# Chunked attention before a squared-ReLU FFN: transposed scores, softmax sums from a ones column, 64x64 matmuls on four tiles, and attention placed at fixed steps of the preceding block's FFN

## Chip, cores and metric

One core of a Trainium2 chip. The metric is the device time of one execution in microseconds (us). Several executions are timed and their median is quoted. Ratios with an interval are the mean time of one kernel's fast runs over the mean of the kernel before's fast runs of the same rounds, so they are not quite the ratio of the medians quoted beside them.

Names: PE is the matrix engine TensorE (PEld its weight loads), DVE is VectorE, ACT is ScalarE, POOL is GpSimd. SP issues the DMAs. A stretch of a profile is written 126.05–158.09, in us from the start of the profiled execution. The granted clock is the share of its full clock that PE was given, as the profile records it; matmuls at half of it are called cold. The head is the time before the FFN runs steadily.

## The reference

```python
# q, k, v: (batch 8, heads 8, sequence 576, dim 64), float32
# chunks of 64 tokens: 9 per sequence; each attends to itself only
scores = matmul(q_c, k_c^T) / sqrt(64)
attn   = exp(scores - max); attn = attn / (sum(attn) + 1e-9)
x      = matmul(attn, v_c)              # -> (4608 tokens, 512)
h      = maximum(x @ w_in, 0)           # w_in  (512, 2048)
out    = (h * h) @ w_out                # w_out (2048, 512), float32 out
```

The FFN is 9 blocks of 512 tokens with 128 matmuls of 128x128 by 128x512 each. Attention is small beside it, but it consists of many small instructions that depend on each other.

## The kernel before

A batch has 576 tokens, and four head pairs. Attention runs in groups: for each head pair one group of eight chunks and one of a single chunk. After each group three queued FFN units are emitted. A scheduler places instructions where the program leaves it a choice.

```python
groups = [(0, 8), (8, 1)]
# ... pools, weights: w_in by DVE/ACT, w_out by GpSimd, cut ...

def attention_group(b, hp, tiles, c0, nch):
    # 8 (or 2) transposes of q and k, then a copy to qkT: cut
    for cc in range(nch):                       # scores, queries on partitions
        nc.tensor.matmul(out=sc_ps[0:64, cc],   lhsT=qkT[0:64, 0, cc],   rhs=qkT[0:64, 1, cc], ...)
        nc.tensor.matmul(out=sc_ps[64:128, cc], lhsT=qkT[64:128, 0, cc], rhs=qkT[64:128, 1, cc], ...)
    nc.scalar.activation(out=attn_exp[:, :nch], in_=sc_ps[:, :nch], func=AF.Exp, scale=scale)
    nc.vector.reduce_sum(out=sums[:, :nch], in_=attn_exp[:, :nch], axis=AXL.X)
    nc.vector.reciprocal(out=rec[:, :nch], in_=sums[:, :nch])
    nc.vector.tensor_tensor(out=attn_n[:, :nch], in0=attn_exp[:, :nch], in1=rec..., op=ALU.mult)
    for cc in range(nch):                       # the weights of attention, turned
        nc.tensor.transpose(out=attnT_ps[0:64, cc * 128:(cc + 1) * 128], in_=attn_n[:, cc], ...)
    nc.vector.tensor_copy(out=attnT[:, :nch], in_=attnT_ps[0:64])
    for cc in range(nch):                       # values, two tiles
        # two 64x64 matmuls into xTo_ps[0:64] and xTo_ps[64:128]: cut
    nc.scalar.copy(out=xT[:, hp, t0:t0 + T], in_=xTo_ps)

# ffn_chunk_units(j): 16 units "4 matmuls w_in, relu, square", then 4 units "16 matmuls w_out, copy, store"

for b in range(B):
    # ... loads, cut ...
    for hp in range(n_hp):
        for (c0, nch) in groups:
            attention_group(b, hp, tiles, c0, nch)
            if hp == n_hp - 1:
                # queue the units of every FFN chunk whose 512 tokens are now complete
                ...
            emit_pending(3)
```

The softmax here doesn't subtract the row's maximum and nothing guards it: scores larger than these inputs give would overflow.

## Time and profile before

| | before |
|---|---|
| time, median of 3 runs | 428.6 us (427.62 to 429.38) |
| profiled span | 427.9 us |
| PE busy, share of the span | 85% |
| mean granted PE clock | 0.931 |
| steady FFN begins (read from the timeline) | about 49 us |
| period: 576 tokens of attention and one FFN chunk | 44.45 us |

The lines of the profile are in the prediction below. The "busy" column counts an engine as busy while one of its instructions is in flight, and matmuls are pipelined, so the 85% does not say that only 15% is to be had. At the 216 ns between starts that the prediction reads from the tail, a block's 128 matmuls take 27.64 us.

### The profile page before, as it was taken

What the parts mean: (1) busy time and instruction counts of PE and PEld (TensorE: products, weight loads), DVE (VectorE), ACT (ScalarE), POOL (GpSimd) and SP (SyncE); (2) the same over time, 40 slices, a digit from 0 to 9 for tenths busy, and PEclk for the clock granted to TensorE, in tenths of its full rate; (3) what the DMA queues carried; (4) which work ended last, traced back from release to release, by engine and by line L of the source; (5) the groups of instructions that cost most, each with busy time, mean ns of one, the idle gap of its engine ahead of it and who ended that gap; (6) DMA issues with size and microseconds to landing.
All of it is one profiled execution on the core that took longest, in us unless ns stands there. A gap on an engine that the chain in (4) does not pass through costs nothing.

```text
span 427.9 us, 7535 instructions
## 1 busy us (share of the span) xinstructions
PE 365.1 (85%) x2862; PEld 184.5 (43%) x2912; DVE 187.0 (44%) x482; ACT 148.3 (35%) x295; POOL 10.9 (3%) x23
## 2 busy tenths in 40 slices
PE   0256699957999799979997999899988999799996
PEld 0234344433445444444444444444444444344442
DVE  2433444344643565256624572447244734440320
ACT  0111262222532263225422542255224523361631
POOL 0003500000000000000000000000000000000000
PEclk9999999965999699979998899979996999699999
DMA  9966860565314741656045524562356011001001
GB/s 271 285 142 221 240 126 28 133 163 127 80 37 122 171 109 25 170 138 146 19 126 141 129 56 116 138 151 54 90 135 147 23 38 64 0 2 74 25 26 74
DMA packets 123812, 46.64 MB, mean 109 GB/s; under 512 B 116608, under 2 KB 116608, under 8 KB 123264
## 3 DMA queue, kind: packets, MB, share of 16 engines
q1 hardware_dynamic: 123200, 41.97, 39.5%
q10 hardware_dynamic: 576, 4.19, 2.6%
q8 instruction: 23, 0.38, 0.4%
q14 instruction: 13, 0.11, 0.1%
HBM read 36.70 MB, written 9.44 MB: 108 GB/s over the span
## 4 chain that ended last, share of the span: by engine, by line
PE 78%; SPq 5%; DVE 5%; DMA 5%; ACT 3%; issue 2%; ACTq 0%
PE hT L204 33%; PE o_ps L219 26%; PE abank L168 6%; PE abank L122 3%; PE abank L138 3%; PE abank L178 3%; PE abank L129 2%; DMA v_sb<-in_v_dram 2%; DMA k_sb<-in_k_dram 2%; DVE attnT L174 2%; DVE attn_n L160 2%; ACT xT L191 2%; PE abank L184 1%; SPq L97 1%; SPq L100 1%
## 5 line engine op out<-in xcount | busy, mean ns | idle before, releaser
L204 PE MATMUL hT<-xT,w_in_bf 128*128 128x512 bf16 x549 | 149.6, 410 | 8.1 <-ACT xT L191 4.3
L219 PE MATMUL o_ps<-w_out_bf,gT 128*128 128x512 bf16 x553 | 133.2, 380 | 1.9 <-issue 0.6
L211 ACT ACTIVATE rl<-hT 128x512 bf16<-128x512 f32 x130 | 77.6, 597 | 72.1 <-PE hT L204 71.1
L212 DVE TENSOR_TENSOR gT<-rl 128x512 bf16<-128x512 bf16 x144 | 59.8, 420 | 68.4 <-ACT rl L211 68.3
L204 PEld LDWEIGHTS <-w_in_bf 128*128 128x128 bf16 x576 | 55.4, 104 | 67.5 <-issue 21.8
L219 PEld LDWEIGHTS <-gT 128*128 128x128 bf16 x576 | 52.1, 98 | 57.1
L135 DVE COPY qkT<-abank 128x1024 bf16<-128x1024 bf16 x64 | 29.0, 454 | 82.5 <-PE abank L129 82.4
L226 ACT COPY o_sb<-o_ps 128x512 f32<-128x512 f32 x36 | 21.1, 585 | 84.9 <-PE o_ps L219 73.2
L168 PE MATMUL abank<-ident_bf,attn_n 128*64 128x128 bf16 x288 | 31.3, 254 | 17.4 <-DVE attn_n L160 17.4
L156 ACT ACTIVATE attn_exp<-abank 128x512 bf16<-128x512 f32 x64 | 26.0, 410 | 54.2 <-PE abank L144 52.6
L191 ACT CAST xT<-abank 128x512 bf16<-128x512 f32 x64 | 24.5, 399 | 52.7 <-PE abank L184 52.7
L174 DVE COPY attnT<-abank 64x1024 bf16<-64x1024 bf16 x64 | 27.9, 447 | 26.6 <-PE abank L168 26.6
L122 PE MATMUL abank<-ident_bf,q_sb 128*128 128x128 bf16 (+1 forms) x160 | 21.0, 239 | 18.1 <-DMA q_sb<-in_q_dram 13.1
L158 DVE TENSOR_REDUCE sums<-attn_exp 128x8 f32<-128x512 bf16 x64 | 28.2, 444 | 17.4 <-ACT attn_exp L156 17.0
L168 PEld LDWEIGHTS <-attn_n 128*64 128x64 bf16 x288 | 22.1, 128 | 30.9 <-DVE attn_n L160 27.7
L160 DVE TENSOR_TENSOR attn_n<-attn_exp,rec 128x512 bf16<-128x512 bf16 x64 | 28.9, 456 | 1.6
L178 PE MATMUL abank<-attnT,v_sb 64*64 64x64 bf16 x288 | 20.8, 210 | 8.4 <-DVE attnT L174 7.8
L122 PEld LDWEIGHTS <-q_sb 128*128 128x128 bf16 (+1 forms) x160 | 13.5, 108 | 30.6 <-issue 23.6
L138 PE MATMUL abank<-qkT 64*64 64x64 bf16 x288 | 21.6, 204 | 5.3 <-DVE qkT L135 5.1
L138 PEld LDWEIGHTS <-qkT 64*64 64x64 bf16 x288 | 14.5, 114 | 22.4 <-DVE qkT L135 20.2
L178 PEld LDWEIGHTS <-v_sb 64*64 64x64 bf16 x288 | 16.2, 122 | 17.7 <-issue 15.6
L129 PE MATMUL abank<-ident_bf,k_sb 128*128 128x128 bf16 (+1 forms) x160 | 22.7, 235 | 0.0
(17 smaller groups left out, 125.3 us busy)
## 6 DMA issues: line engine op xcount, KB each, us to landing
v_sb<-in_v_dram SPq DMA_DIRECT2D x64, 144.0 KB, 3.2
out_dram<-o_sb SPq DMA_DIRECT2D x36, 256.0 KB, 2.1
q_sb<-in_q_dram SPq DMA_DIRECT2D x64, 128.0 KB, 2.8
k_sb<-in_k_dram SPq DMA_DIRECT2D x64, 128.0 KB, 2.9
w_in_stage<-in_moe_w_in_dram ACTq DMA_DIRECT2D x4, 1024.0 KB, 6.6
w_out_stage<-in_moe_w_out_dram SPq DMA_DIRECT2D x16, 256.0 KB, 3.7
q_sb<-in_q_dram SPq DMA_DIRECT2D x64, 16.0 KB, 2.4
k_sb<-in_k_dram SPq DMA_DIRECT2D x64, 16.0 KB, 2.1
```

What stands on the lines that cost most here:

```text
L122: nc.tensor.transpose(out=qkT_ps[:, sg * 128:sg * 128 + tk], in_=q_bfv[0:tk, sg0 + sg, :, 1::2], identity=ident_bf[0:tk, 0:tk],)
L129: nc.tensor.transpose(out=qkT_ps[:, T + sg * 128:T + sg * 128 + tk], in_=k_bfv[0:tk, sg0 + sg, :, 1::2], identity=ident_bf[0:tk, 0:tk],)
L138: nc.tensor.matmul(out=sc_ps[0:64, cc], lhsT=qkT[0:64, 0, cc], rhs=qkT[0:64, 1, cc], start=True, stop=True,)
L160: nc.vector.tensor_tensor(out=attn_n[:, :nch], in0=attn_exp[:, :nch], in1=rec[:, :nch].to_broadcast([128, nch, CH]), op=ALU.mult,)
L168: nc.tensor.transpose(out=attnT_ps[0:64, cc * 128:(cc + 1) * 128], in_=attn_n[:, cc], identity=ident_bf[0:128, 0:128],)
L174: nc.vector.tensor_copy(out=attnT[:, :nch], in_=attnT_ps[0:64])
L178: nc.tensor.matmul(out=xTo_ps[0:64, cc * 64:(cc + 1) * 64], lhsT=v_bfv[:, 0, c, 1::2], rhs=attnT[:, cc, 0], start=True, stop=True,)
L191: nc.scalar.copy(out=xT[:, hp, t0:t0 + T], in_=xTo_ps,)
L204: nc.tensor.matmul(out=hT, lhsT=w_in_bf[:, dt, ft * 128:(ft + 1) * 128], rhs=xT[:, dt, t0:t0 + TCH], start=(dt == 0), stop=(dt == n_dt - 1),)
L211: nc.any.tensor_scalar(out=rl, in0=hT, scalar1=0.0, scalar2=None, op0=ALU.max)
L212: nc.vector.tensor_tensor(out=gT[:, ft, :], in0=rl, in1=rl, op=ALU.mult)
L219: nc.tensor.matmul(out=o_ps, lhsT=gT[:, ft, tt * 128:(tt + 1) * 128], rhs=w_out_bf[:, ft, :], start=(ft == 0), stop=(ft == n_ft - 1),)
```

## The change

The intent, part by part:

- Scores are computed transposed (keys on partitions), so that their exponentials are already the stationary operand of the values matmul. The 36 transposes per 576 tokens of attention's weights go away.
- V gets a 65th column of ones. The values matmul then yields the softmax sum as well. The division comes after it, on 256 elements instead of 512, and the separate sum goes.
- The 64x64 matmuls use all four 64x64 tiles of the PE array, not the two on the diagonal.
- Tokens are taken in blocks of 512, across batches, so the one-chunk groups vanish.
- The order is fixed by hand. Each block's attention is seven steps at fixed places among the 32 FFN steps of the block before it.

The diff at its core (loads, transposes of q and k, and the FFN bodies are cut, and most removed lines with them):

```diff
-    groups = [(0, 8), (8, 1)]
+    ps_ffn = ctx.enter_context(tc.tile_pool(name="ps_ffn", bufs=4, space=bass.MemoryType.PSUM))
+    ps_att = ctx.enter_context(tc.tile_pool(name="ps_att", bufs=2, space=bass.MemoryType.PSUM))
+    ctx.enter_context(tc.manual_schedule())
...
+    v_tiles = [w_pool.tile([128, n_tt, H, D + 1], FP32, name=f"v_sb{i}") for i in range(2)]
+    for vt in v_tiles:
+        nc.gpsimd.memset(vt[:, :, :, D:D + 1], 1.0)
...
+    wst_pool = ctx.enter_context(tc.tile_pool(name="wst", bufs=2))       # load_w_in, load_w_out:
+            eng = nc.vector if h == 0 else nc.gpsimd                      # halves of a w_in tile
+        eng = nc.vector if i % 2 == 0 else nc.gpsimd                      # whole w_out tiles
...
+    def scores(j, r):
+            for hh in range(2):
+                for t in range(n_tt):
+                    for a in range(2):
+                        for p in range(2):
+                            c = p ^ a
+                            o0 = a * 512 + hh * 256 + t * 64
+                            nc.tensor.matmul(
+                                out=ps[64 * c:64 * c + 64, o0:o0 + 64],
+                                lhsT=qkT[64 * a:64 * a + 64, 1, hh, cols],
+                                rhs=qkT[64 * a:64 * a + 64, 0, hh, cols], ...)
+            nc.scalar.activation(out=e..., in_=ps, func=AF.Exp, scale=scale)
+    def values(j, t):
+            for hp in range(n_hp):
+                e = state[j, "e", hp // 2]
+                for a in range(2):
+                    for p in range(2):
+                        c = p ^ a
+                        nc.tensor.matmul(
+                            out=ps[64 * p:64 * p + 64, a, hp * (D + 1):(hp + 1) * (D + 1)],
+                            lhsT=e[64 * c:64 * c + 64, a, hp % 2, t, :],
+                            rhs=vb[64 * c:64 * c + 64, t, 2 * hp + a, 1::2], ...)
+            nc.vector.reciprocal(out=rec, in_=o[:, :, :, D])
+            # x = o * rec, one tensor_tensor for each a
...
+    def attention(j):
+        return [[transpose_qk(j, 0)], [transpose_qk(j, 1)],
+                [scores(j, 0), scores(j, 1)],
+                [values(j, 0), values(j, 1)], [values(j, 2), values(j, 3)],
+                [transpose_x(j, 0)], [transpose_x(j, 1)]]
...
+    load_qk(0); load_v(0)            # then 4x load_w_in, 8x load_w_out, load_qk(1), load_v(1)
+    # attention(0) runs alone, then for every block j:
+        at = [14, 17, 20, 23, 26, 29, 31] if j == 0 else [1, 4, 8, 13, 17, 22, 26]
+        # before FFN step at[i], step i of attention(j + 1) is issued
```

In `scores`, the four matmuls of one turn of the loop over `t` use the tiles (row group, column group) = (0,0), (0,1), (1,1), (1,0). I call them a quad.

## The prediction

> **What bounds the kernel now.** I read the page first, then the tail and one period of the middle in stretches, then the instruction order of both programs. The page:
>
> ```profile
> span 427.9 us, 7535 instructions
> PE 365.1 (85%) x2862; PEld 184.5 (43%) x2912; DVE 187.0 (44%) x482; ACT 148.3 (35%) x295; POOL 10.9 (3%) x23
> ...
> PE   0256699957999799979997999899988999799996
> ...
> PEclk9999999965999699979998899979996999699999
> DMA  9966860565314741656045524562356011001001
> ...
> L204 PE MATMUL hT<-xT,w_in_bf 128*128 128x512 bf16 x549 | 149.6, 410 | 8.1 <-ACT xT L191 4.3
> L219 PE MATMUL o_ps<-w_out_bf,gT 128*128 128x512 bf16 x553 | 133.2, 380 | 1.9 <-issue 0.6
> ```
>
> TensorE is the bound: no other engine passes 44%. But it has gaps in the first five slices (53 us), and the clock row dips about once every four slices. The durations of 410 and 380 ns overlap each other; what a matmul costs is the distance between starts. That comes from the tail, where only FFN runs: four output evacuations start at 414.05, 417.51, 420.96 and 424.46, so 16 matmuls take 3.455-3.47 us, 216 ns each at full clock. 1152 of them are 248.8 us: the floor that the change doesn't touch. About 179 us lie outside it.
>
> The middle repeats every 44.45 us (one batch of 576 tokens and one FFN chunk). Columns of the stretches: length, busy time of PE, PEld, DVE, ACT, POOL with instruction counts, granted clock, DMA share, GB/s.
>
> ```profile
> 227.80:230.00 2.20, 2.20 (x26) 1.00 (x24) 1.64 (x6) 0.70 (x2) 0.00 (x0) 1.00 0.43 145
> 230.00:234.80 4.80, 2.29 (x33) 1.86 (x32) 2.74 (x9) 1.06 (x4) 0.00 (x0) 0.70 0.75 167
> 234.80:238.70 3.90, 3.67 (x14) 1.88 (x15) 1.36 (x3) 1.06 (x3) 0.00 (x0) 0.50 0.37 85
> 238.70:272.25 33.55, 33.18 (x275) 15.96 (x278) 16.14 (x41) 13.93 (x28) 0.00 (x0) 1.00 0.43 104
> ```
>
> For 4.8 us no FFN unit is left (24 slots per batch, 20 units), and attention runs as a bare chain:
>
> ```profile
> 230.96 0.21 PE L144 MATMUL abank<-qkT 64*64 64x64 bf16 x1
> 231.79 1.05 PE L168 MATMUL abank<-ident_bf,attn_n 128*64 128x128 bf16 x9 [0.62 <-DVE attn_n L160]
> 233.50 0.21 PE L178 MATMUL abank<-attnT,v_sb 64*64 64x64 bf16 x1 [0.67 <-DVE attnT L174]
> ...
> 234.81 0.58 PE L204 MATMUL hT<-xT,w_in_bf 128*128 128x512 bf16 x1 [0.62 <-ACT xT L191]
> ```
>
> The clock then stays at half until 238.7. So 44.45 = 27.6 (128 matmuls) + 4.8 (hole) + about 2 (half of the 3.9 cold us) + 10 of attention on PE while warm.
>
> Inside attention the starts give the costs: eight row-tiled 64x64 pairs take 0.05 us for the first step and then 31.7 ns per pair (202.69 to 202.88 in six steps); the start of such a group is about 0.11 us late after FFN, and FFN about 0.10 us late after it: 0.21 us per switch there and back. Four 128x128 transposes take 0.23 us, 57 ns each.
>
> **What the skill says.** "TensorE: Matmul & The Clock Gate", Back-to-back issue gap, gives N/2.4 + 2.5 ns warm: 215.8 at N=512 and 55.8 at 128. The trace agrees (216, 57). The same section's sustained 131 ns for N=512 isn't seen in the tail. Part 1 there: idleness of some 3.4 us halves the clock; seen at 231.9 (0.50 granted). "TensorEngine Tiling (Array Packing)", Tiling Modes, gives four independent 64x64 tiles, and a drain when the mode changes; the 0.21 us is that drain's price here. The clock-gate page's Part 3 says that a weight load overlaps running matmuls only if its row group differs. No trace of before has two tiles of one row group; the new scores have (each quad goes row 0, row 0, row 1, row 1), so this is my main doubt on PE.
>
> **The change part by part.**
>
> *Removed:* per 576 tokens, 36 transposes of the weights of attention, the sum, the normalisation of 128x512 (DVE 0.68 each) and the evacuations between; the one-chunk groups (nine chunks as 8+1), each with its own mode switch; the hole and its cold stretch, since each block's attention is now spread over fixed slots of the preceding block's 32 FFN steps.
>
> *Added per 512 tokens, on PE:* 48 transposes of 128x128 (32 for q and k, 16 for x) x 57 ns = 2.74 us. 128 small matmuls = 32 quads. If a quad costs what a pair did: 1.0 us; if tiles still go two by two: 2.0. I take 50 ns, 1.6 us. Mode switches: scores of both rounds together, values twice, 3 x 0.21 = 0.63. Sum 5.0; with a little waiting, 5.2.
>
> *Does anything hold PE in a steady block of 27.6 + 5.2 = 32.8 us?* ACT: 16 relu x 0.60 + 4 stores x 0.585 + 2 exp of 128x1024 (from 0.223 at 64 and 0.596 at 512 elements, 0.83 ns each, so 1.02) = 14.0. The two exps make a lump of 2.04 us, and four FFN banks hold 3 x 0.86 us: no stall. DVE: 16 squares x 0.42, four copies of 1024 x 0.69, four values (0.2 reciprocal + 2 x 0.42), two xT copies x 0.69 = 15.0. Between values at slots 13 and 17 DVE has 2.1 + 3 x 0.42 = 3.4 us of work in 3.5 us, and the banks come free before the last squares. DMA: 3.15 MB of q, k, v at 225 GB/s (262.00 to 262.50: share 0.98, 225 GB/s) = 14 us, plus 1 MB out, of 32.8. Hidden. So PE alone paces the blocks.
>
> *The head, on the path.* In the new program's DVE order all eight weight casts stand before the first qkT copy. So attention of block 0 waits for nearly all weights. q, k, v first: 1.3 + 14.0 = 15.3 us. w_in, 4 MB through two 1 MB buffers: about 13.5, as w_out took 34.2 to 48 us in before, with 1 MB in flight too; w_out again 14: 43; the last cast, 44. Then bare: two copies 1.4, scores cold 0.9, exps to 4.8, four values paced by DVE at 1.04 each and their first matmuls to 9.5, two x transposes and copies to 11.2. FFN starts at 55 us.
>
> *Sum:*
> - head 55.0
> - block 0: 27.6 + 2.2 cold + 5.2 + 0.9 (the last x transpose is in its last slot, so the copy to xT is waited for) = 35.9
> - blocks 1 to 7: 7 x 32.8 = 229.6
> - block 8, no attention left: 27.6
> - from the last matmul to the end, as in before (424.4 to 427.9): 3.5
> - measured time over profiled span, as in before: 0.7
>
> 352.3; I say 353.
>
> Against before: 7 periods lose about 11.6 us each, 81 us; the two FFN chunks that ran alone at the end now lie over attention, but the last block still does; the head gets some 6 us worse (steady FFN began at 49).
>
> **The rivals.**
>
> 1. *Quads don't overlap.* If same-row tiles serialise, a quad costs 100 to 130 ns: 32 quads are 3.2 to 4.2 us instead of 1.6, 8 blocks: +13 to +21, about 370. For: the row-group sentence. Against: in before, loads of 110 ns already run at 31.7 ns a pair, so loads are deeply pipelined.
> 2. *The head becomes longer.* V rows now lie 65 floats apart, so its 256-byte pieces land at odd addresses; if they cost double, +5 us; staging waits may add 5: 363. For: PE, DVE and ACT all stand idle in it. The other way, if weights stream at the 385 GB/s seen at 228.5, the head is 6 us shorter: 347.
> 3. *The in-order streams of a fixed order couple.* A late exp or values copy now stops FFN too, at seven points a block. 1 us per block gives +8: 361. Against: each consumer is four slots, 3.5 us, behind its producer.
> 4. *It hardly gains* (over 420), if PE's gaps were the same work elsewhere. The 4.8 us hole, the cold 3.9 us and the counts speak against it.
>
> **Range and chances.** The blocks are fixed by 216 ns x 1152; what is open is 4.2 to 7.5 us of attention per block (-8 to +18) and the head (-6 to +9), not all at once. 342 to 368. Even all rivals together stay under 400. Faster 0.98.
>
> **What would show it right or wrong.** Each step has its line: FFN's first matmul near 55 us and DVE's first qkT copy near 44; a period near 32.8 us; PE's row at 9s from slice 7 on and PEclk without dips after the head; small matmuls by fours 30 to 65 ns apart; DMA share near 0.5. Wrong would be: PE waiting each block on ACT exp or DVE x; quads over 100 ns; the clock below 1.00 in mid-run; q and k of a later block arriving late.

## The result and the profile after

| | before | after |
|---|---|---|
| time, median of 4 runs in the same rounds | 428.99 us | 350.84 us (350.12 to 351.37) |
| ratio, 95% interval | | 0.8176 [0.8149, 0.8203] |
| profiled span | 427.9 us | 349.6 us |
| mean granted PE clock in the profiled run | 0.931 (records from 54.5 us on) | 1.000 (records from 63.6 us on) |
| first FFN matmul after which FFN goes on | about 49 us | 58.14 us |
| period | 44.45 us per 576 tokens | 32.04 us per 512 tokens |

The time fell by 18%. The prediction had 353. One of the other three runs lists a mean clock of 0.936 at the same time, 350.60 us, so the two means don't compare whole runs: time without a record counts as full clock.

The page of the changed kernel. The rows of digits are the span in 40 slices of 8.7 us, as tenths of busy time or of clock:

```profile
span 349.6 us, 6592 instructions
PE 293.8 (84%) x2693; PEld 149.9 (43%) x2736; DVE 132.1 (38%) x314; ACT 123.0 (35%) x199; POOL 11.6 (3%) x17
...
PE   0400026999999999999999999999999999999995
...
PEclk9999999999999999999999999999999999999999
...
L240 PE MATMUL ps_ffn<-xT,w_in_bf 128*128 128x512 bf16 x552 | 131.8, 385 | 2.9 <-DVE xT L215 1.6
...
L162 PE MATMUL ps_att<-qkT 64*64 64x64 bf16 x576 | 7.0, 199 | 35.0 <-DVE qkT L147 35.0
```

From slice 7 on (counted from 0), PE's row is all 9s but for the last, and the dips of the clock row are gone. In the slices before, the clock row says nothing: its first record is at 63.6 us, and full clock is printed up to there. The share of busy time is the same as before, 84% against 85%: this column could not have told the gain. What is left of idle time stands in slices 0 to 6. Its largest part is in the last line: 35.0 us in which PE waits for the copy of the transposed q and k.

The changed kernel by stages. Columns: length, busy time of PE, PEld, DVE, ACT and POOL with counts, granted clock, DMA share, GB/s:

```profile
0.00:58.14 58.14, 9.23 (x177) 6.87 (x178) 13.00 (x26) 3.33 (x3) 11.56 (x17) 1.00 0.89 234
58.14:94.01 35.87, 34.45 (x298) 16.85 (x304) 14.35 (x34) 13.34 (x22) 0.00 (x0) 1.00 0.59 124
126.05:158.09 32.04, 31.78 (x301) 16.24 (x305) 13.98 (x34) 13.45 (x22) 0.00 (x0) 1.00 0.60 132
```

The first is the head, the second block 0, and the third a steady block. DVE and ACT are busy 14 of 32 us and DMA 60%, so nothing but PE fills a steady block. All blocks from 1 to 7 last 32.03 to 32.11 us.

The order of PE within that steady block, from the timeline. Columns: start, length, engine, line, operation, names and count:

```profile
132.16 3.62 PE L240 MATMUL ps_ffn<-xT,w_in_bf 128*128 128x512 bf16 x16
135.70 0.71 PE L162 MATMUL ps_att<-qkT 64*64 64x64 bf16 x64
136.34 4.49 PE L240 MATMUL ps_ffn<-xT,w_in_bf 128*128 128x512 bf16 x19
140.77 0.46 PE L182 MATMUL ps_att<-v_sb,e 64*64 64x65 bf16 x32
141.15 1.90 PE L240 MATMUL ps_ffn<-xT,w_in_bf 128*128 128x512 bf16 x7
```

No line has an idle time in brackets, so PE waits for nothing. All 64 scores of a block take 0.64 us from their first start to FFN's next (135.70 to 136.34), 32 of the values 0.38 us. The head, in the same view for DVE:

```profile
47.21 0.69 DVE L124 CAST w_out_bf<-w_out_st 128x1024 bf16<-128x1024 f32 x1 [4.09 <-DMA w_out_st<-in_moe_w_out_dram]
47.82 2.48 DVE L147 COPY qkT<-ps_att 128x1024 bf16<-128x1024 bf16 x4
```

DVE waits in its fixed order for the weights until 47.21. Only then does it copy q and k, which PE had transposed long before. The bare chain of block 0's attention follows, 47.82 to 58.14.

### The profile page after: what moved, and what is told of

It reads as the page before. It is cut to its first block, busy times and chain, and to the rows that moved or that the text cites. A ratio compares the mean times of both kernels' runs of the same rounds, so it can differ in the third digit from the quotient of the medians.

```text
span 349.6 us, 6592 instructions
## 1 busy us (share of the span) xinstructions
PE 293.8 (84%) x2693; PEld 149.9 (43%) x2736; DVE 132.1 (38%) x314; ACT 123.0 (35%) x199; POOL 11.6 (3%) x17
## 4 chain that ended last, share of the span: by engine, by line
PE 82%; DMA 7%; SPq 5%; DVE 3%; issue 1%; ACT 0%; POOL 0%
PE ps_ffn L240 36%; PE ps_ffn L260 36%; DMA w_out_st<-in_moe_w_out_dram 5%; PE ps_att L142 4%; PE ps_att L211 3%; SPq L83 2%; DMA w_in_st<-in_moe_w_in_dram 2%; PE ps_att L182 2%; PE ps_att L162 2%; SPq L102 1%; SPq L95 1%; DVE w_out_bf L124 1%; DVE qkT L147 1%; DVE x L193 1%; POOL w_in_bf L114 0%
## 5 line engine op out<-in xcount | busy, mean ns | idle before, releaser
L240 PE MATMUL ps_ffn<-xT,w_in_bf 128*128 128x512 bf16 x552 | 131.8, 385 | 2.9 <-DVE xT L215 1.6
L260 PE MATMUL ps_ffn<-w_out_bf,gT 128*128 128x512 bf16 x557 | 129.1, 379 | 1.1 <-issue 0.2
L246 ACT ACTIVATE rl<-ps_ffn 128x512 bf16<-128x512 f32 x144 | 85.0, 600 | 59.8 <-PE ps_ffn L240 59.8
L252 ACT COPY o_sb<-ps_ffn 128x512 f32<-128x512 f32 x36 | 20.8, 588 | 110.0 <-PE ps_ffn L260 106.7
L169 ACT ACTIVATE e<-ps_att 128x1024 bf16<-128x1024 f32 x18 | 17.5, 1023 | 53.2 <-PE ps_att L162 53.2
L215 DVE COPY xT<-ps_att 128x1024 bf16<-128x1024 bf16 x18 | 12.5, 692 | 46.9 <-PE ps_att L211 46.9
L193 DVE TENSOR_TENSOR x<-ps_att,rec 128x256 bf16<-128x256 f32 x72 | 27.2, 419 | 1.2
L147 DVE COPY qkT<-ps_att 128x1024 bf16<-128x1024 bf16 x36 | 23.0, 683 | 1.8 <-PE ps_att L142 1.8
L142 PE MATMUL ps_att<-ident,q_sb 128*128 128x128 bf16 x144 | 12.4, 229 | 10.3 <-DMA q_sb<-in_q_dram 10.2
L142 PE MATMUL ps_att<-ident,k_sb 128*128 128x128 bf16 x144 | 12.1, 229 | 0.2 <-DMA k_sb<-in_k_dram 0.2
L211 PE MATMUL ps_att<-ident,x 128*128 128x128 bf16 x144 | 11.7, 229 | 0.5 <-DVE x L193 0.5
```

The costliest lines, as they stand in the source:

```text
L142: nc.tensor.transpose(out=psb[:, c0:c0 + 128], in_=srcb[:, t, 2 * hp:2 * hp + 2, 1::2], identity=ident)
L147: nc.vector.tensor_copy(out=qkT[:, which], in_=psb[:, which * 1024:(which + 1) * 1024])
L169: nc.scalar.activation(out=e.rearrange("p a h t q -> p (a h t q)"), in_=ps, func=AF.Exp, scale=scale)
L193: nc.vector.tensor_tensor(out=x[:, :, a, :], in0=o[:, a, :, 0:D], in1=rec[:, a].to_broadcast([128, n_hp, D]), op=ALU.mult)
L211: nc.tensor.transpose(out=psb[:, c0:c0 + 128], in_=x[:, hp].rearrange("p a d -> p (a d)"), identity=ident)
L240: nc.tensor.matmul(out=h, lhsT=w_in_bf[:, dt, ft * 128:(ft + 1) * 128], rhs=xT[:, dt, :], start=(dt == 0), stop=(dt == n_dt - 1))
```

## The experiments

Twelve kernels ran, beside the kernel before on the same chip. Its medians there were 429.3 to 430.1. "FFN(j)" is the first FFN matmul of block j.

### 1. The same matmuls, paired differently (e1_pairs)

The prediction's main doubt on PE was whether tiles of one row group overlap. The loops are turned so that neighbours in the program are always diagonal tiles, as before the change. Edit against the changed kernel (values likewise):

```diff
-                for t in range(n_tt):
-                    for a in range(2):
-                        for p in range(2):
+                for p in range(2):
+                    for t in range(n_tt):
+                        for a in range(2):
```

> The changed kernel with the 64x64 matmuls reordered so that neighbours use only two tiles at a time (opposite corners of the array), as before; nothing else differs. Theory: in the changed kernel's trace four matmuls start within 10 ns and the next four 31.7 ns later, the price of a pair before, so 32 quads become 64 pairs and each block gains 32 x 31.7 ns = 1.0 us of TensorE: 8 blocks, +8 us, about 359. Rival: the sequencer or the weight loads set the pace, so that pairs cost half a quad and the time stays at 351.

Measured 351.67 us, ratio 0.8182 [0.8159, 0.8206]: unchanged against 350.84. A steady block took 32.18 us instead of 32.04. Timeline of PE:

```profile
135.48 0.80 PE L162 MATMUL ps_att<-qkT 64*64 64x64 bf16 x64
136.21 4.49 PE L240 MATMUL ps_ffn<-xT,w_in_bf 128*128 128x512 bf16 x19
```

The scores take 0.73 us instead of 0.64. My theory, that the order in the program decides how many tiles run at once, fell. The other tiles are eight instructions away in this program. If each pair had waited for the pair before it, 32 pairs at 31.7 ns would have taken 1.0 us and more, as the next experiment shows. If only the starts had kept the program's order, the first pair of one diagonal could have started with the last pair of the other, and only every third round could have had four starts. The records show seven rounds in a row, from 135.56 to 135.76, with four starts within 9 ns each. My reading is that free tiles start early even when their instruction is not next in line.

### 2. Only two tiles (e5_two_tiles)

The same count of matmuls, but all on the two diagonal tiles. The outputs are wrong (relative error 1.04), because the rows land in the wrong places.

```diff
-                            c = p ^ a
-                            o0 = a * 512 + hh * 256 + t * 64
+                            c = a
+                            o0 = p * 512 + hh * 256 + t * 64
...
-                        c = p ^ a
+                        c = p
```

> The changed kernel with scores and values computed on only two of the four tiles (opposite corners); the same number, shape and order of instructions, and a wrong result on purpose. Theory: the reordered run showed that order does not stop TensorE from running four tiles together, but with two tiles in use nothing can overlap beyond a pair: 32 quads become 64 pairs, 32 x 31.7 ns = 1.0 us a block, period 33.05 instead of 32.04 us, +8.5 in all: about 359. Rival: the pace is a cost per instruction (7.9 ns each) whatever the tiles: period stays at 32.0 to 32.2.

Measured 359.83 us, ratio 0.8371 [0.8346, 0.8396], as expected. Blocks took 33.05 us, 1.01 more. Timeline of PE:

```profile
137.56 1.20 PE L162 MATMUL ps_att<-qkT 64*64 64x64 bf16 x64
138.69 4.49 PE L240 MATMUL ps_ffn<-xT,w_in_bf 128*128 128x512 bf16 x19
```

The scores take 1.13 us against 0.64 with four tiles. The difference is 0.49 us, that of 32 rounds against 16 at 31.7 ns (0.51). So a round costs 31.7 ns, whether two or four tiles take part, and the four tiles are worth 1.0 us a block. This is what the number of tiles buys. The order in the program buys little: 0.14 us a block (e1).

### 3. Attention in one lump (e3_lump)

The instructions stay, but all seven steps stand at the last FFN step of a block.

```diff
-        at = [14, 17, 20, 23, 26, 29, 31] if j == 0 else [1, 4, 8, 13, 17, 22, 26]
+        at = [31] * 7
```

> The changed kernel with all seven attention steps of the next block run after the last FFN step of a block, instead of spread over its slots; the same instructions. Theory: the gain rests on the spreading, since a bare attention took 10.3 us in the head (47.8 to 58.1) against 4.4 us of TensorE when spread, and leaves the clock at half for some us (+2): 8 blocks x (5.9 + 2) = +63, about 414, with the clock dipping once a block. Rival: the gain is the smaller work of attention; then waiting is short because exp and copies are quick: below 375.

Measured 420.64 us, ratio 0.9792 [0.9764, 0.982]. The clock row of its page, then one block from the stretches (columns as above), then the end of a lump in PE's timeline (in brackets, the idle time before and what ended it):

```profile
PEclk9999999995999699869986997799779968996899
```

```profile
140.25:181.22 40.97, 35.81 (x301) 18.17 (x304) 14.24 (x34) 13.95 (x22) 0.00 (x0) 0.87 0.49 107
```

```profile
178.50 1.94 PE L211 MATMUL ps_att<-ident,x 128*128 128x128 bf16 x16 [0.47 <-DVE x L193]
181.22 0.58 PE L240 MATMUL ps_ffn<-xT,w_in_bf 128*128 128x512 bf16 x1 [0.78 <-DVE xT L215]
```

A block takes 40.97 us: 27.64 of FFN, 11.2 of the bare chain (its first transpose starts at 170.06, FFN resumes at 181.22), and the remaining 2.1 from the clock, which falls to half in the lump and stays there after it. The time is 6.6 us above the expected 414. Against one lump the placement is worth 420.64 - 350.84 = 69.8 us, and the fewer instructions in one lump gain 2% on the kernel before. That kernel was not lumped, though: it spread its attention too, in the scheduler's order. The new instructions in the scheduler's order were not run.

### 4. Filling the hole of the kernel before, first try (e4_before_filled)

The prediction explained the 4.8 us hole by arithmetic: 24 slots per batch for 20 FFN units. If so, issuing 20 units over the slots closes it. Edit against the kernel before:

```diff
-                emit_pending(3)
+                emit_pending(3 if nch == 8 else 2)
```

> The kernel before with one number changed: 2 FFN units instead of 3 after each one-chunk group, so that 20 units are asked for per batch, as many as there are, instead of 24. Theory: the 4.8 us hole and the 2 us of half clock after it go, 6.8 us in each of 7 periods: about 381. The rest, some 30 us, is then the smaller work of attention. Rival: the hole only moves to other waits in the attention chain: above 415.

Measured 428.6 us, ratio 0.9978 [0.9947, 1.0009]: nothing. PE's timeline around the end of a batch:

```profile
231.67 0.69 PE L168 MATMUL abank<-ident_bf,attn_n 128*64 128x128 bf16 x9 [1.41 <-DVE attn_n L160]
...
234.20 0.38 PE L204 MATMUL hT<-xT,w_in_bf 128*128 128x512 bf16 x1 [0.64 <-ACT xT L191]
```

The hole is still there, with the same waits. The arithmetic was not its cause. The next FFN chunk needs the attention group that is just being computed, and by then nothing older is left to run.

### 5. Filling the hole, second try (e7_before_lag)

If the cause is that nothing older is left, then units must be held back. Here ten stay in reserve:

```diff
-                emit_pending(3)
+                emit_pending(max(0, min(3, len(pending) - 10)))
```

> The kernel before with a reserve: FFN units are handed out only while more than 10 are pending, so that the newest chunk, which needs the attention group just under way, is never the only work left. The run with 2 units instead of 3 failed because the hole is a dependency: nothing older than the new chunk was left. Theory: now the hole and the cold stretch go (6.8 us in 6 periods, 41 us), and some 9 us are paid once for holding units back in the first overlapped batch: about 396, periods near 37.6. Rival: the small matmuls' and copies' latency stalls TensorE in other places of the attention groups: above 415.

Measured 405.36 us, ratio 0.9436 [0.9406, 0.9466], a gain of 23.6 us. One period, from the stretches:

```profile
205.42:246.24 40.82, 39.93 (x346) 18.93 (x350) 22.82 (x59) 16.21 (x33) 0.00 (x0) 1.00 0.46 111
```

The clock is 1.00 throughout and PE is busy 39.93 of 40.82 us: the hole is gone. Yet the period fell only from 44.45 to 40.83 us, by 3.6, where I had expected 6.8 (periods near 37.6, and 396 in all). The attention of 576 tokens therefore costs PE 40.83 - 27.64 = 13.2 us even with no hole (0.9 of it idle), not the 10 that the prediction put down.

### 6. What the removed transposes were worth (e9_transposes_pe)

Two steps are added per block: 16 transposes each of the exponentials, 128x64, with the copies of their results. Nothing uses what they make.

```diff
+    def transpose_again(j, r):
+            for i in range(16):
+                nc.tensor.transpose(out=psb[0:64, i * 128:(i + 1) * 128], in_=e[:, i], identity=ident)
+            # two copies of 64x1024 by nc.vector
...
+        at = ([14, 16, 18, 21, 23, 25, 27, 29, 31] if j == 0
+              else [1, 4, 8, 13, 16, 18, 21, 24, 27])
```

> The changed kernel with the 32 transposes of 128x64 that the old layout needed given back to TensorE for blocks 1 to 8, on its exp tiles, with their four copies of 64x1024 on VectorE; results thrown away. Theory: the blocks are paced by TensorE alone, so they cost 32 x 71 ns = 2.3 us a block (71 ns each in before) and nothing for VectorE's 2.7 us: 8 x 2.3, +18: about 369. Rival: PE has slack and takes them for nothing (351), or VectorE and the banks couple in and it costs more (over 376).

Measured 368.77 us, ratio 0.8576 [0.8556, 0.8596], as expected. Timeline of PE:

```profile
147.98 1.08 PE L226 MATMUL ps_att<-ident,e 128*64 128x128 bf16 x16
149.00 1.90 PE L277 MATMUL ps_ffn<-w_out_bf,gT 128*128 128x512 bf16 x8
```

Sixteen of them take 1.02 us, and a block became 2.23 us longer (34.27 us). The copies on DVE cost nothing beyond that.

### 7. The removed work on DVE (e8_softmax_dve)

The old sum and normalisation are done again on DVE, beside the last two steps: `reduce_sum` and `tensor_tensor` on 128x8x64, twice for each half. Nothing uses them.

```diff
-            [transpose_x(j, 0)],
-            [transpose_x(j, 1)],
+            [transpose_x(j, 0), softmax_again(j, 0)],
+            [transpose_x(j, 1), softmax_again(j, 1)],
```

> The changed kernel with the old softmax work given back to VectorE: per block four sums over 128x512 and four multiplications of 128x512 on the exp tiles, placed beside the two x transposes; results thrown away. In before they took 0.68 and 0.69 us, so 5.5 us a block. Theory: VectorE has 14 of 32 us of work a block and is off the path, so their removal by itself bought nothing: 351, period 32.0. Rival: VectorE's order couples in, and the time rises by over 1%, to 355 or more.

Measured 353.85 us, ratio 0.8242 [0.8219, 0.8265]: 3 us above the 351 expected, and below the rival's 355. A steady block, from the stretches, then the start of FFN(0) in PE's timeline:

```profile
128.95:160.99 32.04, 32.04 (x305) 16.23 (x304) 19.13 (x42) 13.45 (x22) 0.00 (x0) 1.00 0.60 132
```

```profile
60.54 15.22 PE L252 MATMUL ps_ffn<-xT,w_in_bf 128*128 128x512 bf16 x60 [3.12 <-DVE xT L215]
```

DVE has 19.1 us of work in a steady block instead of 14.0, and the block still takes 32.04 us. The 3 us come from the head (FFN(0) 2.4 us later) and from block 0 (0.5 more). The same DVE work is free where PE sets the pace. Where it lies in the chain it is paid: of block 0's share, the half that DVE does before the last copy to xT (some 2.6 us, an estimate: half of the 5.1 us that a steady block got) delays FFN(0) by 2.4 us.

### 8. What a change between tile shapes costs (e12_six_groups)

Scores and values are issued in six separate groups instead of three, each with FFN before and after.

```diff
-            [scores(j, 0), scores(j, 1)],
-            [values(j, 0), values(j, 1)],
-            [values(j, 2), values(j, 3)],
+            [scores(j, 0)], [scores(j, 1)],
+            [values(j, 0)], [values(j, 1)],
+            [values(j, 2)], [values(j, 3)],
```

(with `at` = 1, 4, 8, 9, 13, 14, 17, 18, 22, 26 in the steady blocks)

> The changed kernel with its small matmuls in six groups a block instead of three (each round of scores and each tile of values in its own FFN slot); the same instructions. Theory: each return trip between FFN and 64x64 matmuls costs 0.21 us on TensorE, so 3 more of them are 0.63 us a block, period 32.67, +5 in all: about 356. Rival: the gap before a group is the latency of one group's start, hidden behind FFN: 351.

Measured 356.4 us, ratio 0.8304 [0.8283, 0.8325], as expected. Blocks took 32.72 us, 0.68 more for three more trips to the small tiles and back: 0.225 us each. The prediction had 0.21 from the trace of before.

### 9. The head: casts off DVE (e2_casts_on_pool)

All weight casts go to GpSimd, so that DVE can copy q and k of block 0 at once.

```diff
-            eng = nc.vector if h == 0 else nc.gpsimd
+            eng = nc.gpsimd
...
-        eng = nc.vector if i % 2 == 0 else nc.gpsimd
+        eng = nc.gpsimd
```

> The changed kernel with the casts of all weights on GpSimd instead of half of them on VectorE. Theory: the 58 us head is VectorE's order (eight weight casts stand before the first qkT copy), not the data, so attention of block 0 ends near 25 us and FFN starts there; block 0 then waits in its slot 14 for q and k of block 1 (landing near 58 us) and ends near 78 instead of 94: about 335. Rival: transfers bound the head anyway (weights land until 50 us), and FFN of block 0 just waits for them: 348 to 351.

Measured 340.06 us, ratio 0.7923 [0.7887, 0.7959], 5 us above what I expected. Timeline of PE:

```profile
24.92 14.45 PE L240 MATMUL ps_ffn<-xT,w_in_bf 128*128 128x512 bf16 x57 [0.22 <-issue]
52.15 0.37 PE L142 MATMUL ps_att<-ident,q_sb 128*128 128x128 bf16 x2 [12.78 <-DMA q_sb<-in_q_dram]
...
81.10 1.90 PE L240 MATMUL ps_ffn<-xT,w_in_bf 128*128 128x512 bf16 x8 [0.79 <-DVE xT L215]
```

FFN(0) begins at 24.09 instead of 58.14, 34 us earlier. FFN(1) begins at 81.10 instead of 94.01, only 12.9 earlier. In between, PE waits for q of block 1, whose transfer stands behind all of w_out. The wait has moved from DVE's order to the order of transfers.

### 10. The head: order of transfers and more staging (e6_head)

e2 with four staging buffers for weights instead of two, and q and k of block 1 ahead of w_out.

```diff
-    wst_pool = ctx.enter_context(tc.tile_pool(name="wst", bufs=2))
+    wst_pool = ctx.enter_context(tc.tile_pool(name="wst", bufs=4))
...
+    load_qk(1)
     for i in range(8):
         load_w_out(i)
-    load_qk(1)
     load_v(1)
```

> The run with all casts on GpSimd, and in addition q and k of block 1 are loaded ahead of w_out, and the staging pool has 4 buffers instead of 2. Theory: in that run block 0 stood 12.8 us on q of block 1, queued behind w_out, and then PE went on at half clock; with the new order q and k land near 40 us, w_out near 53, and FFN of block 1 starts near 62 to 66 instead of 81: about 320 to 326. Rival: w_out then comes too late for the second half of block 0 and the wait only moves: 335 or more.

Measured 328.06 us, ratio 0.7626 [0.7603, 0.7649], slightly above what I expected. Timeline of PE:

```profile
44.84 3.57 PE L260 MATMUL ps_ffn<-w_out_bf,gT 128*128 128x512 bf16 x8 [1.32 <-POOL w_out_bf L124]
...
68.53 1.90 PE L240 MATMUL ps_ffn<-xT,w_in_bf 128*128 128x512 bf16 x8 [0.79 <-DVE xT L215]
```

The long wait is gone and FFN(1) begins at 68.53. What is left is many short waits (3 us for q and k, 1.3 here, about 1 for v). The run changes the order and the buffers at once, so it doesn't say which of them gave how much.

### 11 and 12. Two more orders of the head (e10_best, e11_split)

Both are e6 with another order. e10 brings all of block 1's q, k, v before w_out, and runs its attention bare in the middle of block 0:

```diff
+    load_qk(1)
+    load_v(1)
     for i in range(8):
         load_w_out(i)
...
+        at = [14] + [15] * 6 if j == 0 else [1, 4, 8, 13, 17, 22, 26]
```

> The head run changed once more: q, k and v of block 1 before w_out, and attention of block 1 all at the end of the first half of block 0, where TensorE waits for w_out anyway. Theory: q and k land near 42 us, v near 47, w_out from 48 to 58, so that the second half runs right behind w_out and FFN of block 1 starts near 62 instead of 68.5: about 321.5. Rival: the second half loses as much by waiting for w_out as attention gains: 327 or more.

e11 puts v between the halves of w_out:

```diff
+    load_qk(1)
+    for i in range(4):
+        load_w_out(i)
     load_v(1)
+    for i in range(4, 8):
+        load_w_out(i)
...
+        at = [14, 15, 19, 23, 24, 26, 28] if j == 0 else [1, 4, 8, 13, 17, 22, 26]
```

> As the run before it, but v of block 1 between the two halves of w_out, and attention of block 1 spread over slots 14 to 28 of block 0. Theory: the sum of bytes before FFN of block 1 (14.7 MB, done near 58 us) is the bound in both, so FFN of block 1 starts near 61 to 63 here too, 320 to 322. Rival: order matters: this and the other differ by over 1%.

Measured 329.75 us, ratio 0.7679 [0.7647, 0.7711] for e10, and 327.93 us, 0.7638 [0.7615, 0.7661] for e11. Both missed what I expected. Timelines of PE, e10 then e11:

```profile
52.00 1.94 PE L211 MATMUL ps_att<-ident,x 128*128 128x128 bf16 x16 [0.47 <-DVE x L193]
53.73 14.82 PE L260 MATMUL ps_ffn<-w_out_bf,gT 128*128 128x512 bf16 x64
68.58 0.59 PE L240 MATMUL ps_ffn<-xT,w_in_bf 128*128 128x512 bf16 x2
```

```profile
59.03 1.86 PE L260 MATMUL ps_ffn<-w_out_bf,gT 128*128 128x512 bf16 x4 [5.68 <-POOL w_out_bf L124]
...
69.10 1.89 PE L240 MATMUL ps_ffn<-xT,w_in_bf 128*128 128x512 bf16 x8
```

FFN(1) begins at 68.53, 68.58 and 69.10 us in the three orders, though PE waits for quite different things in them. My expectation rested on v and w_out having landed by 58 us. In e10 the last cast of w_out ended at 63.6.

What the three orders have in common is the bytes that must arrive before FFN(1): q, k and v of two blocks (6.3 MB) and the weights (8.4 MB). I first took their sum for the bound of all three, but e10's trace speaks against it. There PE runs the 64 w_out matmuls from 53.73 to 68.58 without a wait, all but the first five 216 ns apart. What sets that start is the bare attention of block 1 from 44.21 to 53.73, itself behind q and k, whose last piece PE waits for until 42.3. In e11 PE does stand 5.68 us on the second half of w_out. So the starts are near each other for different reasons. No run changed the number of bytes, and what would bring FFN(1) forward stays open.

e6 and e11 are the fastest kernels found, 6.5% below the changed kernel and equal to each other. All kernels but e5 gave correct results.

## Why the prediction was right

The time was right (353 against 350.84), and so was the mechanism: PE alone paces the blocks, the rest is hidden, and the head is set by the weight casts in DVE's order. The terms of its sum against the trace of the changed kernel:

| term | predicted, us | measured, us |
|---|---|---|
| head, to FFN(0) | 55.0 | 58.14 |
| block 0 | 35.9 | 35.87 |
| blocks 1 to 7 | 7 x 32.8 = 229.6 | 224.3 (318.33 - 94.01) |
| block 8 | 27.6 | 27.8 |
| after the last matmul | 3.5 | 3.5 |
| span | 351.6 | 349.6 |
| measured time over the span | 0.7 | 1.2 (350.84 - 349.6) |

Two errors cancel. Block 0's exact agreement is luck as well: its attention was reckoned 0.8 us too dear, and its cold start too cheap (13 matmuls took 5.49 us from 58.14 to 63.63, 2.7 more than at 216 ns each; 2.2 had been put down).

**The head was 3.1 us too short.** The last DVE cast ended at 47.9, not at 44. The delay is there before the first weights: by the prediction's sum the first w_in tile was there at 18.7 (15.3 for q, k, v and 3.4 for a quarter of w_in), and DVE cast it at 22.57. The issues of the DMAs on SP (start, length, as before), then a stretch from the later part of v's:

```profile
8.62 1.10 SPq L95 DMA_DIRECT2D v_sb<-in_v_dram  x1
...
17.05 10.10 SPq L109 DMA_DIRECT2D w_in_st<-in_moe_w_in_dram  x4
```

```profile
14.00:16.00 2.00, 0.70 (x7) 0.43 (x5) 0.00 (x0) 0.00 (x0) 0.00 (x0) 1.00 0.59 133
```

SP takes from 8.62 to 17.05, 8.4 us, to issue the 1 MB of v in twelve DMAs, and only then reaches w_in, 1.8 us later than the 15.3 of the sum. The 2 MB of q and k before took it 7.9 us. Until about 13 us the DMA engines are full (share over 1 from 8.62 to 13); in the stretch shown they are at 0.59, so there they are not what is slow. The prediction had reckoned v by bytes, at 225 GB/s, and missed the count of its DMAs. No run merged them, so this reading rests on the trace alone. The other 2.1 us are in the first w_in tile: it is cast 5.5 us after its issue began, and 3.4 had been put down. Why it took so long stays open. From then on the working held within 0.4 us (24.6 us from the first w_in cast on DVE to the last of w_out, 24.3 from 18.7 to 43 in the prediction). The bare chain was 10.3 us and not 11.2, which gave 0.9 back. The dependence itself held: moving the casts (e2) took FFN(0) to 24 us.

**The blocks were 5.3 us too long.** Attention on PE cost 32.04 - 27.64 = 4.40 us a block, not 5.2. The mis-sized term is the quad: 50 ns had been chosen between 31.7 and 63. Measured, a round is 31.7 ns with two or four tiles (e5), so 16 rounds of scores are 0.51 us, and values cost about the same. The 57 ns of a transpose and the 0.21 us of a trip were right (55.6 ns, and 0.225 from e12).

**Rival 1, same-row tiles serialising, is out.** Quads go row 0, row 0, row 1, row 1, and a round still costs what a diagonal pair costs. The Trainium skill, "TensorE: Matmul & The Clock Gate", Part 3, says that a weight load overlaps running matmuls only when the row group differs. Here loads of 112 ns stand behind rounds of 31.7 ns, with two tiles of each row group in every round, so the measurement decides against the sentence for 64x64 tiles. (Another sentence of that Part allows an early load into the background weight buffer too. Whether that is at work here no run shows.)

**Rival 2, a longer head through v, came true in part:** the head is longer, by 3.1 us, and v's issues are the likely cause of 1.8. Odd addresses are not: in the stretch of v above, 133 GB/s at a share of 0.59 are 225 GB/s at full share, what the kernel before had at 0.98. **Rival 3, coupled streams, did not happen:** e8 put 5 us more work on DVE in each block without moving the period. **Rival 4 is out:** the gain is 18%.

**Where the text was wrong.** Its split of the 44.45 us period had two wrong terms. It gave the reason for the hole as "24 slots per batch, 20 units"; e4 shows that this isn't it, and e7 that a reserve of older units is. And it put 4.8 + 2 us to the hole and the cold clock and 10 to attention. The hole contains useful attention work as well (2.29 us of PE busy time in its 4.8). Removing it gained 3.6 us a period, and attention costs 13.2. This did no harm, because the prediction built the new time from the new kernel's own terms and used the old split only as a check. It also says that idleness of some 3.4 us was seen to halve the clock at 231.9. What the trace shows is the fall; in the 3.41 us before it (228.59–232.00) PE was busy for 2.18.

**Where the 78 us came from.** If the steady part of before begins at 49 us, it is 49 + 7 x 44.45 + 67.7 = 427.9, and after is 58.1 + 224.3 + 67.1 = 349.6. The head lost 9 us, seven periods gained 87, and what is left (two blocks and the end) stayed. Of those 87, some 25 are the hole with its cold clock (7 x 3.6, and e7 gained 23.6 as a whole). The rest is PE work, in part only because a period holds 576 tokens. Per 512 tokens, attention on PE fell from 13.2 x 8/9 = 11.7 to 4.4 us, by 7.3. The transposes of the weights are 2.2 of it (e9), and four tiles instead of two 1.0 (e5). That leaves 4.1 us. Trips between tile shapes are the likely rest: in e7's period, from which the 13.2 comes, PE's timeline changes its tile shape some 57 times (the transposes of the weights, 128x64, and of the one-chunk groups, 64x128, count as shapes of their own), in a steady block after 6 times. At e12's 0.225 us for a trip of two changes this would be 5.0 us per 512 tokens, an estimate and more than is left, so some changes must cost less or the parts overlap (e9's 2.23 is 0.45 more than 32 transposes at 55.6 ns, so two such trips may be in it). No run separates them. The sum and normalisation taken off DVE are worth nothing in steady blocks (e8).

Nearly all of this is lost without the spreading: in one lump (e3) the same lean attention takes 11.2 us of mostly waiting, and the gain is 2%.

## What to carry to other kernels

Where one engine has a large independent stream of work, place the small dependent chain at points of that stream far enough apart for each link to finish, and keep older work in reserve for the moments when the newest depends on the chain: here the same instructions ran 70 us faster so placed than in one lump, and in the kernel before a reserve alone gained 23.6, while the share of busy time did not move (85% before, 84% after). Put a fixed order under suspicion at the start of the program, where one slow transfer in an engine's order holds everything behind it. When such a wait is removed, look for the next one, here in the order of transfers, before counting the gain (34 us earlier became 13). Price small matmuls by the rounds over the tiles in use and by the trips between tile shapes, not by their own durations.

## What the Trainium skill lacked or had wrong

- "TensorE: Matmul & The Clock Gate", Part 3: a weight load is said to overlap only if the row group differs, and matmuls to start strictly in order. Quads with two tiles of each row group cost 31.7 ns, as a diagonal pair did. With the order changed so that only diagonal pairs are neighbours (e1), seven rounds in a row, from 135.56 to 135.76 us, had four starts within 9 ns each. With starts in program order only every third round could have.
- The same page, Part 4: about 275 ns for a 128x128 transpose in a kernel is the duration of one, as the 229 ns in the trace here are, and no spacing is given. What one costs in a row is less: eight take 0.45 us by their starts, 55.6 ns each, and one of 128x64 takes 64 ns by the starts of 16 (1.02 us) or 70 ns by the period.
- "TensorEngine Tiling (Array Packing)", Tiling Modes: a change of mode drains the array, without a figure. A trip to 64x64 tiles and back costs 0.225 us (three more per block: 0.68).
- "DMA: Bandwidth & Descriptors", Bandwidth: the share lost to 256-byte pieces is worked out there as 27% for the fixed cycles; the descriptor metadata is named beside them without a share. The DMA engines being busy at shares of 0.98 and above, 256-byte pieces moved 225 GB/s (262.00–262.50 of the kernel before) and weight rows of 2 KB 390 to 394 (20–28 us of e6): some 42% less.
- "TensorE: Matmul & The Clock Gate", Part 1, warns that clock events in a trace can be unreliable; no page says that their beginning can be missing. In the changed kernel the first record is at 63.6 us and 1.00 is printed before it, while the twelve matmuls from 58.94 on start 426 ns apart and the next ones 217. e9, with the same order of casts in its head, has 0.50 on record from 17.7 to 62.1.
